# An attention and soft-MoE kernel whose first 27 microseconds are put in another order

## The chip, the cores and the metric

The kernel runs on one core of a Trainium2 chip. A core has a matrix engine (TensorE, here PE, with its weight loads shown apart as PEld), a vector engine (VectorE, DVE), a scalar engine (ScalarE, ACT), GpSimd (POOL) and a queue (SyncE, SP) from which this kernel issues all its transfers. The five run on their own and meet only at semaphores; each takes its own instructions strictly in the order written. The metric is the device time of one execution in microseconds (us), the median of several runs.

## The reference

Eight batches with eight heads of 576 tokens and 64 channels: causal attention with a decay, and then a soft mixture of experts on its output.

```python
scores = scale * q @ k.T
cum    = cumsum(log(clip(f, 1e-4, 1)))
scores = where(causal, -1e9, scores + cum[:, None] - cum[None, :])
attn   = softmax(scores, -1)
x      = concat_heads(attn @ v)                 # 4608 x 512
logits = x @ phi                                # 32 slots, 4 for each of 8 experts
slots  = softmax(logits, 0).T @ x               # dispatch
slots  = relu(slots @ w1[e]) @ w2[e]            # each expert its own 4 slots
out    = softmax(logits, 1) @ slots             # combine
```

## The kernel before

**Tiling.** Two heads of one batch make a pair; there are 32 pairs (numbered g), 64 heads (numbered i), and 5 blocks of 128 tokens for each head. The transposed q and k of a pair come in one load, `RAW` (three buffers, `load_qk`). A product in float32 is made of rounded parts: `round_k` and `round_q` (ACT, lines L183 and L188) write the rounded values of one head to `WA` and `YA`; `dup_k` and `dup_q` copy these to the other half of the partitions of `WB` and `YB` by transfers inside the core (L199, L203); `low_k` and `low_q` (POOL, L209, L214) write what the rounding lost beside them. `WA` and `YA` have three buffers (pairs g, g+3, ... share one), `WB` and `YB` two. The rows 64 and up of `WA` hold the running sum of log f, rounded and its rest; those of `YA` hold constants and, last, the row maximum. For later pairs the sums go to memory (`cumd`, L581) and come back with `load_cum` (L194).

**A head's way.** `s1` (PE, L230) makes the scores with queries on the partitions, into one of three PSUM buffers `s`; `tops` (DVE, L243) masks them and takes each query's maximum. `mturn` (PE, L253) and `mrows` (ACT copy L262, then a transfer L265) turn the maxima into a row of `YA`. `s2` (PE, L280 and L281) makes the scores again, with keys on the partitions and the maximum taken off, into a ring of three PSUM banks; `expo` (ACT, L287) takes the exponential into `PTS`; `causal` (POOL, L295 and L298) zeroes what the mask forbids, the first instruction for three blocks on the diagonal and two more for the last two. `s3` (PE, L313) multiplies with the values `V`; `norm` (DVE, L328 to L333) divides into `X`; `px` and `xcopy` (PE L340, ACT L376 and L349) transpose that for the logits.

**The order of the work** is written out by hand, engine by engine, by the order of the calls; nothing reorders it. A loop over g from 1 to 31 (L722) is one slot for each pair. In slot g, pair g has `s2`, `expo`, `causal` and `s3`, heads 2g+3 and 2g+4 (u0, u1) have `s1` and `tops`, POOL makes the `low` parts of pair g+1, transfers duplicate pair g+2, and ACT rounds pair g+3 (four casts: two heads, k and q). On ACT a slot's order is: three `expo` of the first head, two `xcopy`, its last `expo`, the first `expo` of the second head, three `xcopy`, two `expo`, the `mrows` copy, the last `expo`, and then the four roundings.

**The opening**, L535 to L688, does by hand what the slots before would have done: the running sum (DVE, L562), pairs 0 to 3 rounded, heads 0 to 4 through `s1` and `tops` (`first(i, n)`, n from 0 to 3 for four groups of blocks), pair 0 through everything. The maxima of heads 0 and 1 take their own way (`first_rows`, L603 and L606). `warm(n, ...)` (L527) issues n matmuls whose result nobody reads.

## Time and profile before

| | |
|---|---|
| median of 3 runs | 390.36 us (390.32 to 391.53) |
| the profiled execution | 391.48 us, of which 389.8 us from its first to its last instruction |
| PE busy | 370.1 us (95%) |
| DVE, ACT, POOL busy | 297.5, 269.9, 251.6 us (76%, 69%, 65%) |
| mean granted clock of TensorE | 0.982 |

Times in the trace are microseconds from the first instruction. A row of a timeline gives the start, the length, the engine, the line, what is written and read, how many instructions are merged in it, and in brackets how long the engine was idle before and what ended that. A row of the windows gives busy time and instructions of each engine in a stretch, the granted clock, the share of the transfer engines and the rate. An engine that is busy all the time in a stretch sets that stretch's length; one that is idle may still be the one for which the others wait.

### The profile page before, as it was taken

To read this page: it belongs to the slowest core of one execution; us is meant where nothing else is said; L and a number is where in the kernel's file an instruction comes from. 1 tells how busy PE (TensorE), PEld (TensorE's weight loads), DVE (VectorE), ACT (ScalarE), POOL (GpSimd) and SP (SyncE) were. 2 spreads that over 40 slices of the span, in tenths; PEclk is the share of its full clock that TensorE was granted. 3 is DMA by queue.
4 is the path that set the end of the run, shared out by engine and by line. 5 is a ranking of instruction groups with operands and counts; after the bars stand their busy time and mean duration, and the time that the engine had idled before them with its cause. 6 is when DMAs were issued, how large, how long until landed. Compare 5 with 4: busy or idle time off the path is not lost.

```text
span 389.8 us, 15241 instructions
## 1 busy us (share of the span) xinstructions
PE 370.1 (95%) x5881; PEld 327.9 (84%) x5881; DVE 297.5 (76%) x1161; ACT 269.9 (69%) x685; POOL 251.6 (65%) x339
## 2 busy tenths in 40 slices
...
GB/s 206 230 153 161 172 189 208 200 199 243 243 197 224 216 236 218 218 209 216 215 211 215 215 213 213 220 208 220 211 183 159 309 341 385 409 408 373 270 358 345
DMA packets 34120, 93.72 MB, mean 240 GB/s; under 512 B 4234, under 2 KB 10048, under 8 KB 34048
## 3 DMA queue, kind: packets, MB, share of 16 engines
...
## 4 chain that ended last, share of the span: by engine, by line
PE 79%; DMA 11%; POOL 3%; ACT 3%; DVE 2%; issue 1%; DVEq 0%; SPq 0%; ACTq 0%; POOLq 0%
PE pv L313 25%; PE ring L280 14%; PE ring L281 12%; PE s L230 11%; DMA w<-in_w 7%; PE pv L340 4%; PE lg L387 2%; PE ds L490 2%; POOL YB L214 1%; DMA out<-p 1%; DMA RAW<-in_qk 1%; PE pv L969 1%; PE ring L490 1%; ACT PTS L287 1%; DMA out<-RAW 1%
## 5 line engine op out<-in xcount | busy, mean ns | idle before, releaser
L287 ACT ACTIVATE PTS<-ring 128x320 f32<-128x320 f32 (+2 forms) x256 | 118.1, 502 | 50.2 <-PE ring L281 39.8
L243 DVE CUSTOM_DVE_ANT_0 s<-s,mask 128x320 f32<-128x320 f32 (+4 forms) x320 | 138.5, 452 | 6.1 <-PE s L230 1.0
L280 PE MATMUL ring<-YA,WA 67*128 67x320 f32 (+9 forms) x384 | 119.5, 325 | 0.0
L281 PE MATMUL ring<-YB,WB 128*128 128x320 f32 (+4 forms) x384 | 110.7, 296 | 0.0
L313 PE MATMUL pv<-V,PTS 128*64 128x65 f32 x3200 | 101.9, 223 | 0.9 <-POOL PTS L295 0.5
L209 POOL TENSOR_TENSOR WB<-RAW,WB 64x576 fp32r<-64x576 f32 x64 | 91.0, 1423 | 15.9 <-DMA YA<-V 5.3
L313 PEld LDWEIGHTS pv<-V,PTS 128*64 128x64 f32 x3200 | 97.1, 138 | 4.7 <-issue 1.2
L230 PE MATMUL s<-WA,YA 66*128 66x288 f32 (+9 forms) x384 | 100.4, 317 | 0.4 <-DVE MT L243 0.3
L214 POOL TENSOR_TENSOR YB<-RAW,YA 64x576 fp32r<-64x576 f32 x64 | 89.7, 1420 | 2.5
L280 PEld LDWEIGHTS ring<-YA,WA 67*128 67x128 f32 (+3 forms) x384 | 68.9, 181 | 5.3 <-issue 1.6
L281 PEld LDWEIGHTS ring<-YB,WB 128*128 128x128 f32 (+1 forms) x384 | 69.9, 182 | 0.0
L230 PEld LDWEIGHTS s<-WA,YA 66*128 66x128 f32 (+1 forms) x384 | 63.0, 191 | 5.3 <-DVE MT L243 0.5
L243 DVE DVE_READ_ACCUMULATOR2_ANT MT<- 128x1 f32 x372 | 52.7, 142 | 0.0
L298 POOL TENSOR_SCALAR_AFFINE_SELECT PTS<-PTS 128x128 f32<-128x128 f32 (+1 forms) x128 | 31.3, 265 | 29.9 <-ACT PTS L287 26.4
L295 POOL TENSOR_SCALAR_AFFINE_SELECT PTS<-PTS 128x384 f32<-128x384 f32 x64 | 33.3, 520 | 18.2 <-ACT PTS L287 14.1
L183 ACT CAST WA<-RAW 64x576 fp32r<-64x576 f32 x64 | 40.0, 669 | 4.0 <-DMA RAW<-in_qk 3.4
L340 PE MATMUL pv<-cs,X 128*128 128x128 f32 x155 | 42.1, 273 | 0.6 <-DVE X L333 0.6
L188 ACT CAST YA<-RAW 64x576 fp32r<-64x576 f32 x64 | 40.0, 669 | 0.4
L243 DVE CUSTOM_DVE_ANT_0 s<-s,mask,MT 128x288 f32<-128x288 f32 x62 | 32.6, 526 | 9.6 <-PE s L230 1.0
L333 DVE TENSOR_TENSOR X<-pv,rl 128x320 f32<-128x320 f32 (+1 forms) x65 | 31.5, 486 | 2.4 <-DMA V<-in_v 0.3
L376 ACT COPY XTS<-pv 128x128 f32<-128x128 f32 (+1 forms) x93 | 25.3, 307 | 1.1 <-PE pv L340 0.8
L340 PEld LDWEIGHTS pv<-cs,X 128*128 128x128 f32 x155 | 21.9, 142 | 1.5 <-DVE X L333 0.9
...
## 6 DMA issues: line engine op xcount, KB each, us to landing
...
```

The source lines that it names most:

```text
L183: nc.scalar.copy(WA[g % 3][0:64, S * h : S * h + S], RAW[g % 3][64:128, h])
L188: nc.scalar.copy(YA[g % 3][0:64, h, 64:640], RAW[g % 3][0:64, h])
L209: nc.gpsimd.tensor_tensor(t[0:64], RAW[g % 3][64:128, h], t[64:128].bitcast(F32), op=ALU.subtract)
L214: nc.gpsimd.tensor_tensor(YB[g % 2][64:128, h], RAW[g % 3][0:64, h], YA[g % 3][0:64, h, 64:640].bitcast(F32), op=ALU.subtract)
L230: nc.tensor.matmul(t[:, o : o + w], ya[0:m, h, 128 * blk : 128 * blk + 128], wa[0:m, j0 : j0 + w], start=True, stop=True)
L243: nc.vector.tensor_tensor_reduce(out=t[:, o : o + w], in0=t[:, o : o + w], in1=mask[:, m0 : m0 + w], scale=1.0, scalar=top if n == 3 else ...
L280: nc.tensor.matmul(o, wa[0:m, j0 : j0 + n], ya[0:m, h, 64 + i0 : 64 + i0 + w], start=True, stop=False)
L281: nc.tensor.matmul(o, wb[:, j0 : j0 + n], yb[:, h, i0 : i0 + w], start=False, stop=True)
L287: nc.scalar.activation(PT[i % 2][:, SEG_O[bank] : SEG_O[bank] + at], t[:, 0:at], AF.Exp, scale=0.125)
L295: nc.gpsimd.affine_select(d3, d3, pattern=[[0, 3], [1, 128]], compare_op=ALU.is_ge, fill=0.0, base=0, channel_multiplier=-1)
L313: nc.tensor.matmul(pvv[h][64 * u : 64 * u + 64, t, :], PT[h][:, at : at + 64], V[:, g % 2, c, 65 * h : 65 * h + 65], start=(c == 0), stop= ...
L340: nc.tensor.transpose(pm[:, 0:128], x[:, t, 128 * (p % 2) : 128 * (p % 2) + 128], ident)
```

## The change

Only the opening and slots 1 and 2 differ; from slot 3 on the programs are the same. The constants for `YA` and `WA` are prepared in `XTS` in place of `V`. For head 1 the two rows of running sums go to `WA` by two transfers in place of two ACT copies. The roundings of pair 1's first head are done together and early, those of its second head inside pair 0's `expo`; pairs 1 and 2 are duplicated head by head, pair 1's first head right behind `load_v(0)`. `load_qk(3)` is issued later. `first(2, ...)` and `first(3, ...)` are put between products of pair 0; `s3` of pair 0 is cut into four parts with `first(3, 2)`, `first(3, 3)` and `first(4, 0)` between. `low_q(2)` comes ahead of `causal(1)`. The last two groups of head 4 and the four roundings of pair 3 move into slot 1, `own_j` (two DVE instructions) into slot 2. Three of the 24 `warm` matmuls are left out.

```diff
-    fill = V.rearrange("p a t c -> p (a t c)")[:, 0:1280].bitcast(F32R)
+    fill = XTS[:, 0:1280].bitcast(F32R)
...
+    def fills(m, n):
+        if n == 0:
+            nc.sync.dma_start(WA[m][66:67].bitcast(F32), fill[0:1, 0 : 2 * S].bitcast(F32))
+        else:
+            nc.sync.dma_start(YA[m][64:66].rearrange("c h s -> c (h s)").bitcast(F32), fill[32:34].bitcast(F32))
+
     nc.vector.tensor_copy(fp[lane, 0:S], fz)
+    nc.sync.dma_start(WA[0][64:65, S:].bitcast(F32), fp[96:97, 0:S].bitcast(F32))
+    dup_k(0, 1, 2)
+    fills(1, 0)
...
+    nc.sync.dma_start(WA[0][96:97, S:].bitcast(F32), fp[96:97, S:].bitcast(F32))
+    for c in range(2):
+        nc.sync.dma_start(WA[1][64 + c : 65 + c].bitcast(F32), fp[65:98:32, S * c : S * c + S].bitcast(F32))
+    fills(1, 1)
+    nc.scalar.copy(WA[0][64:65, 0:S], fp[64:65, 0:S])
     round_q(0, 1)
-    nc.scalar.activation(fin[:, 0:1], ones[:, 0:1], AF.Exp)
     dup_q(0, 1, 2)
+    nc.sync.dma_start(cumd.rearrange("b a c s -> (b a) (c s)"), fp[lane].bitcast(F32))
+    fills(2, 0)
+    fills(2, 1)
     load_qk(2)
     load_v(0)
+    nc.scalar.activation(fin[:, 0:1], ones[:, 0:1], AF.Exp)
...
     round_k(1, 0)
+    round_q(1, 0)
+    dup_k(1, 0, 1)
+    dup_q(1, 0, 1)
...
-    first(1, 1, 3 * WARM[1])
+    first(1, 1, 2 * WARM[1])
+    first(1, 2)
     next(r0)
-    warm(2 * WARM[1], cs)
     next(r0)
-    round_q(1, 0)
-    first(1, 2)
+    round_k(1, 1)
+    first(1, 3, WARM[1])
     both(0, 0)
-    first(1, 3)
+    first(2, 0)
     both(0, 1)
+    round_q(1, 1)
+    dup_k(1, 1, 2)
+    dup_q(1, 1, 2)
...
     causal(0)
     low_k(2)
+    low_q(2)
+    first(2, 3, 2 * WARM[1])
     both(1, 0)
...
     both(1, 3)
+    round_k(2, 0)
+    round_q(2, 0)
+    dup_q(2, 0, 1)
+    dup_k(2, 0, 1)
     causal(1)
-    low_q(2)
     low_k(3)
     low_q(3)
+    s3(0, alone[0][:13])
+    first(3, 2)
+    s3(0, alone[0][13:])
+    first(3, 3)
     nc.vector.memset(most, -1.0e30)
-    s3(0, alone[0])
+    s3(0, alone[1][:13])
     first(4, 0)
+    s3(0, alone[1][13:])
     mturn(1, 1, 2)
     mrows(1, 1, 2)
+    round_k(2, 1)
+    round_q(2, 1)
+    dup_q(2, 1, 2)
+    dup_k(2, 1, 2)
     first(4, 1)
     norm(0)
     load_cum(3)
-    round_k(3)
-    round_q(3)
...
         expo(h0, 0)
+        if g == 1:
+            first(4, 2)
         norm(h0 - 1)
...
         expo(h0, 1)
+        if g == 1:
+            first(4, 3)
...
         expo(h0, 2)
+        if g == 1:
+            round_k(3, 0)
+            round_q(3, 0)
         px(g - 1, 0)
...
         expo(h1, 0)
+        if g == 1:
+            round_k(3, 1)
+            round_q(3, 1)
```

How this stands on the engines, at the three places that matter below. First POOL, from the end of pair 0's `causal(0)` (the last `PTS` row of 64 columns) on; `WB_88`, `YB_87` are the low parts of pair 1, `PTS` the exponentials. Before:

```order
L209 TENSOR_TENSOR WB_88<-RAW_96,WB_88 64x576
L295 AFFINE_SELECT PTS<-PTS 128x3x128
L298 AFFINE_SELECT PTS<-PTS 128x128
L298 AFFINE_SELECT PTS<-PTS 128x64
L214 TENSOR_TENSOR YB_87<-RAW_96,YA_85 64x576
```

and now:

```order
L209 TENSOR_TENSOR WB_88<-RAW_96,WB_88 64x576
L214 TENSOR_TENSOR YB_87<-RAW_96,YA_85 64x576
L295 AFFINE_SELECT PTS<-PTS 128x3x128
L298 AFFINE_SELECT PTS<-PTS 128x128
L298 AFFINE_SELECT PTS<-PTS 128x64
```

The q part of head 2 has moved ahead of head 1's mask. Second ACT, from the last two `expo` of head 1 to slot 1's copies of `X` (`WA_94`, `YA_93` are pair 2, `WA_90`, `YA_89` pair 3, `mr_1` the maxima of head 3). Before:

```order
L287 ACTIVATE PTS<-ring_151 128x512
L188 CAST YA_93<-RAW_97 64x576 x2
L262 CAST mr_1_408<-pv_148 5x128
L183 CAST WA_90<-RAW_95 64x576 x2
L188 CAST YA_89<-RAW_95 64x576 x2
L287 ACTIVATE PTS<-ring_149 128x448
L287 ACTIVATE PTS<-ring_150 128x320
L287 ACTIVATE PTS<-ring_151 128x320
L376 COPY XTS<-pv_147 128x128 x2
L287 ACTIVATE PTS<-ring_149 128x512
L287 ACTIVATE PTS<-ring_150 128x448
L376 COPY XTS<-pv_148 128x2x128
```

and now, from the maxima of head 3 on:

```order
L262 CAST mr_1_430<-pv_148 5x128
L183 CAST WA_94<-RAW_97 64x576
L188 CAST YA_93<-RAW_97 64x576
L287 ACTIVATE PTS<-ring_149 128x448
L287 ACTIVATE PTS<-ring_150 128x320
L287 ACTIVATE PTS<-ring_151 128x320
L183 CAST WA_90<-RAW_95 64x576
L188 CAST YA_89<-RAW_95 64x576
L376 COPY XTS<-pv_147 128x128 x2
L287 ACTIVATE PTS<-ring_149 128x512
L287 ACTIVATE PTS<-ring_150 128x448
L183 CAST WA_90<-RAW_95 64x576
```

The four casts of pair 3 stood ahead of slot 1's first `expo`, and stand among its `expo` now; behind the copy of head 3's maxima there are two casts of pair 2. Third PE, the end of the opening up to slot 1's first product (`YA_85`, `WA_86` with L280). Before:

```order
L313 MATMUL pv_147<-V,PTS 64x65 x25
L230 MATMUL s_0_402<-WA_94,YA_93 128x320
L230 MATMUL s_0_402<-WA_94,YA_93 128x192
L253 MATMUL pv_148<-cs,MT_113 5x128
L230 MATMUL s_1_413<-WA_94,YA_93 128x288
L313 MATMUL pv_148<-V,PTS 64x65 x13
L230 MATMUL s_2_429<-WA_94,YA_93 128x288
L230 MATMUL s_3_436<-WA_94,YA_93 128x448
L230 MATMUL s_3_436<-WA_94,YA_93 128x64
L313 MATMUL pv_148<-V,PTS 64x65 x12
L280 MATMUL ring_149<-YA_85,WA_86 128x448
```

and now:

```order
L313 MATMUL pv_148<-V,PTS 64x65 x13
L230 MATMUL s_0_412<-WA_94,YA_93 128x320
L230 MATMUL s_0_412<-WA_94,YA_93 128x192
L313 MATMUL pv_148<-V,PTS 64x65 x12
L253 MATMUL pv_148<-cs,MT_113 5x128
L230 MATMUL s_1_437<-WA_94,YA_93 128x288
L280 MATMUL ring_149<-YA_85,WA_86 128x448
L281 MATMUL ring_149<-YB_87,WB_88 128x448
L230 MATMUL s_2_452<-WA_94,YA_93 128x288
```

The transposition of head 3's maxima (L253) stood between the values of head 0 and those of head 1, and stands behind both now; the last products of head 4 follow slot 1's first product.

## The prediction

> **What bounds the kernel now.** I read the busy time by stretches cut at the slots' starts first, then the timelines of PE, POOL, ACT and SP over the first 55 us.

> ```profile
> 26.80:36.90 10.10, 9.32 (x147) 8.51 (x143) 8.36 (x35) 7.31 (x18) 9.70 (x12) 1.00 0.62 161
> 36.90:45.70 8.80, 8.77 (x144) 8.38 (x143) 7.20 (x30) 7.16 (x18) 7.95 (x11) 1.00 0.61 169
> ```

> The columns behind the length are PE, PEld, DVE, ACT and POOL, the clock, the transfers' share and rate. In slot 2 PE is busy 8.77 of 8.80 us: PE sets it and, with 95% of the whole span, what follows; whatever shifts slot 2 shifts everything behind it. In slot 1 (26.8 to 36.9) PE lacks 0.8 us and POOL is busy 9.7 of 10.1. So the change is worth what it does to the start of slot 2. PE's timeline up to there:

> ```profile
> 10.38 0.53 PE L230 MATMUL s<-WA,YA 97*128 97x320 f32 x2
> 18.37 0.50 PE L280 MATMUL ring<-YA,WA 98*128 98x448 f32 x1
> 23.09 0.51 PE L230 MATMUL s<-WA,YA 66*128 66x320 f32 x2
> 23.43 0.27 PE L253 MATMUL pv<-cs,MT 128*5 128x128 f32 x1
> 24.21 1.26 PE L313 MATMUL pv<-V,PTS 128*64 128x65 f32 x26 [0.37 <-POOL PTS L295]
> 25.41 0.63 PE L230 MATMUL s<-WA,YA 66*128 66x288 f32 x3
> 25.97 0.92 PE L313 MATMUL pv<-V,PTS 128*64 128x65 f32 x24
> 26.82 0.47 PE L280 MATMUL ring<-YA,WA 67*128 67x448 f32 x1
> 28.96 0.33 PE L340 MATMUL pv<-cs,X 128*128 128x128 f32 x1 [0.59 <-DVE X L333]
> 33.33 1.50 PE L313 MATMUL pv<-V,PTS 128*64 128x65 f32 x42
> 35.00 1.96 PE L313 MATMUL pv<-V,PTS 128*64 128x65 f32 x58 [0.17 <-POOL PTS L295]
> 36.89 0.47 PE L280 MATMUL ring<-YA,WA 67*128 67x448 f32 x1
> 45.66 0.47 PE L280 MATMUL ring<-YA,WA 98*128 98x448 f32 x1
> ```

> Slot 1 starts at 26.82, slot 2 at 36.89, slot 3 at 45.66: slot 1 takes 10.07 us, slot 2 8.77. At 24.21 and again at 35.00 PE waits for POOL's mask, at 28.96 for `norm`. POOL's rows say why the mask is late:

> ```profile
> 9.83 1.41 POOL L209 TENSOR_TENSOR WB<-RAW,WB 64x576 fp32r<-64x576 f32 x1 [5.31 <-DMA YA<-V]
> 11.31 1.41 POOL L214 TENSOR_TENSOR YB<-RAW,YA 64x576 fp32r<-64x576 f32 x1
> 22.16 1.40 POOL L209 TENSOR_TENSOR WB<-RAW,WB 64x576 fp32r<-64x576 f32 x1 [5.12 <-DMA YB<-YA]
> 23.64 0.52 POOL L295 TENSOR_SCALAR_AFFINE_SELECT PTS<-PTS 128x384 f32<-128x384 f32 x1
> 34.42 0.52 POOL L295 TENSOR_SCALAR_AFFINE_SELECT PTS<-PTS 128x384 f32<-128x384 f32 x1
> ```

> It stands idle 5.12 us before `low_k(2)` at 22.16, which needs `dup_k(1)`; a `low` part takes 1.48 from start to start (9.83, 11.31). PE follows a mask's start by 0.57 (23.64 to 24.21) or 0.58 (34.42 to 35.00).

> **The change part by part.** First the duplicate. ACT and SP now:

> ```profile
> 7.20 1.36 ACT L583 CAST WA<-PTS 1x576 fp32r<-1x576 f32 x2
> 9.40 0.67 ACT L188 CAST YA<-RAW 64x576 fp32r<-64x576 f32 x1
> 11.61 0.67 ACT L183 CAST WA<-RAW 64x576 fp32r<-64x576 f32 x1
> 5.81 0.52 SPq L199 DMA_DIRECT2D WB<-WA  x1
> 12.90 0.58 SPq L174 DMA_DIRECT2D RAW<-in_qk  x1
> 17.96 0.48 SPq L199 DMA_DIRECT2D WB<-WA  x1
> 0.80 2.75 DMA PTS<-in_f
> 15.73 3.96 DMA RAW<-in_qk
> ```

> With two of three row copies gone, ACT reaches `round_q(0,1)` at 7.20 + 0.68 = 7.9 instead of 9.4; pair 1's first head, at 11.61 before, is rounded by 11.5 in both parts. SP now decides. From `dup_k(0,0)` at 5.81 to `load_qk(2)` at 12.90 it issues 11 transfers, 0.645 each; `dup_k(1,0)` is the 15th behind the same start, so it is issued at 5.81 + 15 x 0.645 = 15.5 at the latest, and at 14.8 with 0.6 for each: I take 15.2, for the longest of the steps before held waits. `load_qk(2)` itself slips from 12.90 to some 14.1; its first reader, a cast, stands behind head 1's last `expo`, so nothing waits.

> How long the transfer takes has two rows: `dup_k(0,0)`, 5.81 to 9.83, 4.0 us, and `dup_k(1)`, 17.96 to 22.16, 4.2 us, both behind loads. An early end is the 2.75 us of the first load, which had the queue to itself; a late one adds up what is ahead: `load_qk(2)` (576 KB, as the load at 15.73) lands 3.96 after its issue, at 18.1, and behind it come 325 KB and the duplicate's own 144 KB. The transfer engines are nearly full there already (0.87, at 273 GB/s, the last two columns):

> ```profile
> 18.00:20.00 2.00, 2.00 (x15) 1.90 (x14) 1.72 (x9) 1.46 (x3) 0.00 (x0) 1.00 0.87 273
> ```

> At that rate these 469 KB are 1.7 us: 19.8. So the duplicate lands between 18.0 and 19.8; I take 15.2 + 4.2 = 19.4, the row that is nearest in kind. `low_k(2)` then starts 2.76 us earlier than at 22.16.

> [...]

> Of these 2.76 us `causal(1)` gets only part, since `low_q(2)` now stands ahead of it: 19.4 + 2 x 1.48 = 22.35 against 23.64, and PE may go on with head 1's values at 22.35 + 0.57 = 22.9 against 24.21. PE is there by then: `s2` of head 1 starts with the copies of head 1's maxima, now 0.67 later by the cast put in before them:

> ```profile
> 16.51 0.73 ACT L606 CAST YA<-ring 2x512 fp32r<-2x512 f32 x2 [0.16 <-PE ring L603]
> 23.79 0.25 ACT L262 CAST mr<-pv 5x128 fp32r<-5x128 f32 x1 [0.17 <-PE pv L253]
> 25.33 1.25 ACT L188 CAST YA<-RAW 64x576 fp32r<-64x576 f32 x2
> 27.53 1.31 ACT L287 ACTIVATE PTS<-ring 128x448 f32<-128x448 f32 x3 [0.95 <-PE ring L281]
> 29.68 0.43 ACT L376 COPY XTS<-pv 128x128 f32<-128x128 f32 x2 [0.84 <-PE pv L340]
> 30.75 1.03 ACT L287 ACTIVATE PTS<-ring 128x512 f32<-128x512 f32 x2 [0.64 <-PE ring L281]
> 31.67 0.38 ACT L376 COPY XTS<-pv 128x256 f32<-128x256 f32 x1
> 32.38 0.77 ACT L287 ACTIVATE PTS<-ring 128x320 f32<-128x320 f32 x2
> ```

> 16.51 + 0.73 + 0.67 = 17.9, and from there to the end of head 0's values the same work took 18.37 to 23.09, 4.72: 22.6. From 24.21 to 26.82, 2.61 us, PE did head 1's values and two groups of head 4 (25.41 to 25.97, 0.56); these go, and the first group (23.09 to 23.43, 0.34), the transposition (0.03) and the second group (0.14) come: 2.56. **Slot 1 starts at 22.9 + 2.56 = 25.5, 1.4 us earlier.**

> Slot 1 then gives it back on ACT. Before, ACT had rounded pair 3 by 26.6 (25.33 + 1.25) and stood idle 0.95 us when `expo(2,0)` came at 27.53. Now the copy of head 3's maxima waits for a transposition that stands behind all of head 1's values, and two casts of pair 2 are queued behind the copy. The transposition starts at 22.9 + 1.20 + 0.34 + 0.85 = 25.3 and the copy follows by 0.36 (23.43 to 23.79): 25.65. Then in order: the copy 0.25, two casts 1.25, three `expo` 1.31, two casts 1.25, two copies 0.43, two `expo` 1.03, two casts 1.25, three copies 0.71 (31.67 to 32.38), two `expo` 0.77. That is 8.25 us, 8.33 with the 0.01 or so between two, without a wait: 33.98. Before, ACT waited 0.84 and 0.64 for PE inside this slot (29.68, 30.75); the added casts stand just there and fill most of it. I take 0.3 for what is left, with bounds of 0 and 0.9: 34.28. The mask follows at once, POOL being through by 33 (five `low` parts of 1.48 and `causal(2)` behind `causal(1)`): start 34.28, PE goes on 0.58 later at 34.86 where it was 35.00. **Slot 2 starts 0.14 us earlier than at 36.89**; with the bounds of the landing and of ACT's waits, from 0.7 earlier to 0.9 later.

> What costs nothing, and what covers it: `own_j` in slot 2

> ```profile
> 22.65 0.94 DVE L672 TENSOR_SCALAR own_j<-own_j 128x4 f32<-128x4 f32 x1
> 35.80 0.17 DVE L328 TENSOR_SCALAR rl<-pv 128x5 f32<-128x5 f32 x1 [0.96 <-PE pv L313]
> 44.67 0.17 DVE L328 TENSOR_SCALAR rl<-pv 128x5 f32<-128x5 f32 x1 [0.82 <-PE pv L313]
> ```

> stands, with a shorter instruction ahead of it, 1.2 us in all, where DVE waited 0.82 us for the values; the other 0.4 moves `norm(4)`, whose reader on PE comes some 1.5 us into the slot. Without that cover it would cost 1.2. `first(4,2)` and `first(4,3)` cost slot 1 0.56 us of PE, which waits there for ACT anyway, and on DVE at most 1.8 (a slot's 7.20 hold eight such groups and two `norm`); DVE starts on the slot 1.4 earlier and waited 0.96 behind it (35.80). Head 1's two row transfers, issued at about 7.0 and 8.9 by SP's pace, land by 11.6 with the 2.75 us of the first load and could hold PE's `s1` of head 1, at 10.38 before, for 1.2; DVE, which reads it, is busy with head 0 for about half of that, so I count 0.6 at most, and the 0.3 between PE's 22.6 and POOL's 22.9 hide half. The three `warm` matmuls stood where PE waits anyhow. The sum against the profile's own 391.48 is -0.14, which gives 391.3; that run is 0.3% above the median of the runs, so the forecast is 390.36 - 0.14, **390.2 us**, no change: a measurement of this kernel can tell 0.3%, 1.2 us.

> **The rivals.** *PE sets slot 1.* If ACT's waits vanish and its casts hide, slot 1 takes PE's own 8.77 + 0.56 = 9.3 us from 25.5: slot 2 at 34.8, 2.1 earlier, **388.3 us**. For it speaks that ACT had 0.95 + 0.84 + 0.64 = 2.4 us idle about slot 1, nearly the 2.5 that it gets; against it, that the 0.95 lay before `expo(2,0)`, where ACT now waits for the maxima's copy.

> *ACT sets slots 1 and 2.* The landing at 19.8 and waits of 0.9 put slot 2 at 37.9; ACT then ends its last `expo` and the four roundings of pair 4 at about 38.9, and slot 2's first `expo` starts 1.0 behind its product. It decides from the point where that `expo` ends after PE's want of the bank for the fourth product, some 1.8 us into the slot; then PE waits 0.5 more: 1.5 later, **391.8 us**. For it speaks that ACT's 7.16 us in slot 2 leave 1.6 to catch up, and no more; against it, that the landing must be at its late end.

> *The row transfers are late.* Head 1's `s1` starts 0.6 later and the chain to 22.6 with it: 0.3 us lost, 390.5, the same verdict.

> **How the numbers follow.** ACT's chain as summed 0.55, PE sets slot 1 0.24, ACT sets two slots 0.17, late rows 0.04. The forecast's own range, 0.7 earlier to 0.9 later, is 389.7 to 391.3; I widen it to hold the faster rival and stop short of the slower: 388.2 to 391.7. Faster by over 0.3% (below 389.2): the second with 0.02 of the first, 0.26; slower: 0.17; within 0.3%: 0.57.

> **What would show it.** `low_k(2)` at 19.4 (18.0 to 19.8), `causal(1)` at 22.4, slot 1's first product at 25.5; ACT idle from about 22 until the copy of head 3's maxima near 25.7; no more than 0.3 us idle on ACT from there to its last `expo` of slot 1; PE's stop for the mask in slot 1 longer than 0.17; slot 2 at 36.8 and slots 2 and 3 unchanged in length. Wrong if ACT's casts find idle time (slot 1 near 9.3 us), if `low_k(2)` still waits past 20, or if slot 2 is longer than 8.8.

## The result and the profile after

| | before | changed |
|---|---|---|
| median | 391.53 us (390.32 to 400.96, 11 runs) | 394.57 us (392.58 to 395.82, 11 runs) |
| ratio | | 1.0087, 95% interval 1.0064 to 1.0109: slower |
| profiled execution | 391.48 us, span 389.8 | 395.82 us, span 394.1 |
| mean granted clock of that execution | 0.982 | 0.972 |

The forecast was 390.2 us, no change, with a range up to 391.7; the kernel became 0.9% slower and lies outside it. Part of the distance is no term of the prediction: the forecast started from 390.36, the median of three runs, and the kernel before took 391.53 in these eleven. Runs more than 1.5% above the fastest of their kernel are left out of the ratios: 400.96 and 399.50 here, and one of e20_thin below, 398.43. The runs of the changed kernel differ from each other by the clock: the three with a mean granted clock of 0.982 or more took 392.6 to 393.1 us, the eight others, at 0.972 to 0.981, 394.3 to 395.8. So two things have to be found: some 1.1 to 1.6 us that are lost at full clock, and up to 3 us more that come with a lower clock.

PE's timeline of the changed kernel at the places that answer to those shown of before:

```profile
24.05 1.26 PE L313 MATMUL pv<-V,PTS 128*64 128x65 f32 x26 [0.75 <-POOL PTS L295]
26.78 0.37 PE L280 MATMUL ring<-YA,WA 67*128 67x448 f32 x1
28.57 0.40 PE L230 MATMUL s<-WA,YA 66*128 66x288 f32 x1 [1.08 <-ACT YA L188]
37.03 4.99 PE L313 MATMUL pv<-V,PTS 128*64 128x65 f32 x100
41.95 0.47 PE L280 MATMUL ring<-YA,WA 67*128 67x448 f32 x1
```

Head 1's values start at 24.05 (22.9 was predicted, 24.21 before), slot 1 at 26.78 (25.5; 26.82), slot 2 at 41.95 (36.75; 36.89). The opening gained nothing, and slot 1 takes 15.2 us in place of 10.1. At 28.57 stands a stop of 1.08 us that the prediction did not have: `s1` of head 5 waits for a cast of pair 2. And a hundred products for the values take 4.99 us, where in other executions below they take 3.14. The windows, cut at steps of the clock, show why (columns as before; the ninth number, 0.50, is the granted clock):

```profile
27.43:30.84 3.41, 2.33 (x17) 2.09 (x17) 3.23 (x17) 2.70 (x6) 2.91 (x3) 1.00 0.35 75
30.84:34.25 3.41, 3.41 (x17) 3.17 (x16) 2.75 (x13) 3.00 (x7) 1.49 (x4) 0.50 0.82 265
34.25:37.66 3.41, 3.41 (x26) 3.16 (x27) 2.27 (x9) 2.79 (x9) 1.27 (x2) 0.50 0.07 28
37.66:41.07 3.41, 3.41 (x68) 3.41 (x66) 0.63 (x5) 2.62 (x5) 3.05 (x4) 0.50 0.55 107
```

TensorE runs at half clock from 30.84 to 41.07, three windows of 3.41 us, all with PE busy to the last. The window ahead of them holds the stop of 1.08 us. Before, the clock was 1.00 here, from 26.80 to 45.70.

Of the 5.06 us by which slot 2 is late, 4.3 are left at the end (394.1 against 389.8): the execution before had a half-clock window of its own, 3.41 us at 324.38, which the changed one had not.

POOL and SP show where the opening's gain went:

```profile
20.54 1.41 POOL L209 TENSOR_TENSOR WB<-RAW,WB 64x576 fp32r<-64x576 f32 x1 [2.55 <-PE ring L281]
22.00 1.41 POOL L214 TENSOR_TENSOR YB<-RAW,YA 64x576 fp32r<-64x576 f32 x1
23.48 0.52 POOL L295 TENSOR_SCALAR_AFFINE_SELECT PTS<-PTS 128x384 f32<-128x384 f32 x1
```

```profile
14.26 0.39 SPq L174 DMA_DIRECT2D RAW<-in_qk  x1
14.70 0.43 SPq L178 DMA_DIRECT2D V<-in_v  x1
15.24 0.48 SPq L199 DMA_DIRECT2D WB<-WA  x1
```

The duplicate is issued at 15.24, as predicted, but POOL starts `low_k(2)` at 20.54 and not at 19.4. The name behind the arrow is of an operation long done: the wait is for the duplicate, which by its semaphore landed at 20.37, 5.1 us after its issue. And ACT in front of slot 1:

```profile
26.88 0.26 ACT L262 CAST mr<-pv 5x128 fp32r<-5x128 f32 x1 [4.37 <-PE pv L253]
27.16 0.67 ACT L183 CAST WA<-RAW 64x576 fp32r<-64x576 f32 x1
27.84 0.67 ACT L188 CAST YA<-RAW 64x576 fp32r<-64x576 f32 x1
28.42 0.53 ACT L287 ACTIVATE PTS<-ring 128x448 f32<-128x448 f32 x1
```

ACT stands idle 4.37 us for the maxima of head 3, and the two casts of pair 2 that had no need to wait are queued behind: the second ends at 28.5, and with it PE's stop. DVE waits as well. `tops` (L243) of the last two groups of head 3 starts at 20.99 and 21.43 before, the first of them behind 0.20 us in which DVE waits for the product of L230; in the changed kernel at 21.83 and 23.34, behind 1.25 and 0.93 us of waiting for L230.

With parts of pair 0's values ahead of the score products of heads 3 and 4, DVE waits for these products, and the last group comes 1.9 us later.

### The profile page after: what moved, and what is told of

Same layout as the page of the kernel before. It is cut to its first block, busy times and chain, and to the rows that moved or that the text cites. A ratio compares the mean times of both kernels' runs of the same rounds, so it can differ in the third digit from the quotient of the medians.

```text
span 394.1 us, 15235 instructions
## 1 busy us (share of the span) xinstructions
PE 372.8 (95%) x5875; PEld 330.0 (84%) x5875; DVE 297.7 (76%) x1161; ACT 269.1 (68%) x683; POOL 252.1 (64%) x339
## 4 chain that ended last, share of the span: by engine, by line
PE 84%; DMA 6%; ACT 3%; issue 1%; POOL 1%; DVE 1%; SPq 0%; DVEq 0%; ACTq 0%; POOLq 0%
PE pv L313 24%; PE ring L280 14%; PE ring L281 12%; PE s L230 11%; PE pv L340 4%; PE pv L987 3%; PE lg L387 2%; PE ds L490 2%; PE ring L950 2%; PE pv L950 2%; DMA YA<-mr 2%; DMA YB<-YA 1%; ACT PTS L287 1%; DMA out<-p 1%; PE ring L987 1%
## 5 line engine op out<-in xcount | busy, mean ns | idle before, releaser
L287 ACT ACTIVATE PTS<-ring 128x320 f32<-128x320 f32 (+2 forms) x256 | 118.5, 502 | 53.0 <-PE ring L281 38.9
L243 DVE CUSTOM_DVE_ANT_0 s<-s,mask 128x448 f32<-128x448 f32 (+4 forms) x320 | 138.6, 451 | 9.6 <-PE s L230 4.5
L280 PE MATMUL ring<-YA,WA 67*128 67x320 f32 (+9 forms) x384 | 120.4, 327 | 0.6 <-DMA YA<-mr 0.4
L281 PE MATMUL ring<-YB,WB 128*128 128x320 f32 (+4 forms) x384 | 111.8, 299 | 0.0
L313 PE MATMUL pv<-V,PTS 128*64 128x65 f32 x3200 | 103.7, 225 | 1.1 <-POOL PTS L295 0.8
L230 PE MATMUL s<-WA,YA 66*128 66x288 f32 (+9 forms) x384 | 102.0, 321 | 1.6 <-ACT YA L188 1.1
L313 PEld LDWEIGHTS pv<-V,PTS 128*64 128x64 f32 x3200 | 98.8, 140 | 4.7 <-issue 1.2
L209 POOL TENSOR_TENSOR WB<-RAW,WB 64x576 fp32r<-64x576 f32 x64 | 91.1, 1423 | 13.6 <-DMA WB<-WA 6.0
L214 POOL TENSOR_TENSOR YB<-RAW,YA 64x576 fp32r<-64x576 f32 x64 | 89.7, 1420 | 2.4
L280 PEld LDWEIGHTS ring<-YA,WA 67*128 67x128 f32 (+3 forms) x384 | 69.8, 183 | 6.2 <-issue 1.6
L281 PEld LDWEIGHTS ring<-YB,WB 128*128 128x128 f32 (+1 forms) x384 | 70.9, 185 | 0.0
L230 PEld LDWEIGHTS s<-WA,YA 66*128 66x128 f32 (+1 forms) x384 | 64.1, 193 | 7.1 <-ACT YA L188 1.4
L243 DVE DVE_READ_ACCUMULATOR2_ANT MT<- 128x1 f32 x372 | 52.5, 141 | 0.0
L295 POOL TENSOR_SCALAR_AFFINE_SELECT PTS<-PTS 128x384 f32<-128x384 f32 x64 | 33.5, 523 | 22.0 <-ACT PTS L287 16.9
L183 ACT CAST WA<-RAW 64x576 fp32r<-64x576 f32 x64 | 40.2, 669 | 3.3 <-DMA RAW<-in_qk 2.5
L340 PE MATMUL pv<-cs,X 128*128 128x128 f32 x155 | 42.4, 274 | 0.0
L243 DVE CUSTOM_DVE_ANT_0 s<-s,mask,MT 128x288 f32<-128x288 f32 x62 | 32.6, 526 | 11.0 <-PE s L230 2.9
L188 ACT CAST YA<-RAW 64x576 fp32r<-64x576 f32 x64 | 40.2, 669 | 0.4
L333 DVE TENSOR_TENSOR X<-pv,rl 128x320 f32<-128x320 f32 (+1 forms) x65 | 31.5, 486 | 2.4 <-DVE rl L329 0.3
L376 ACT COPY XTS<-pv 128x128 f32<-128x128 f32 (+1 forms) x93 | 25.2, 306 | 0.3
L340 PEld LDWEIGHTS pv<-cs,X 128*128 128x128 f32 x155 | 22.1, 143 | 0.7
```

Of the source, the lines that this page charges most:

```text
L183: nc.scalar.copy(WA[g % 3][0:64, S * h : S * h + S], RAW[g % 3][64:128, h])
L188: nc.scalar.copy(YA[g % 3][0:64, h, 64:640], RAW[g % 3][0:64, h])
L209: nc.gpsimd.tensor_tensor(t[0:64], RAW[g % 3][64:128, h], t[64:128].bitcast(F32), op=ALU.subtract)
L214: nc.gpsimd.tensor_tensor(YB[g % 2][64:128, h], RAW[g % 3][0:64, h], YA[g % 3][0:64, h, 64:640].bitcast(F32), op=ALU.subtract)
L230: nc.tensor.matmul(t[:, o : o + w], ya[0:m, h, 128 * blk : 128 * blk + 128], wa[0:m, j0 : j0 + w], start=True, stop=True)
L243: nc.vector.tensor_tensor_reduce(out=t[:, o : o + w], in0=t[:, o : o + w], in1=mask[:, m0 : m0 + w], scale=1.0, scalar=top if n == 3 else ...
```

## The experiments

All numbers: median, and ratio to the kernel before on the same chip with its 95% interval. The rows come from several chips, so rows are compared by their ratios. "Changed" means that the edit is made to the changed kernel.

| label | edit | median us | ratio |
|---|---|---|---|
| e2_maxima | changed, head 3's maxima ahead of head 1's values | 397.02 | 1.0173 (1.0143 to 1.0204) |
| e3_mask | changed, `causal(1)` ahead of `low_q(2)` | 393.58 | 1.0084 (1.0054 to 1.0114) |
| e10_casts | changed, pair 2's casts ahead of the maxima's copy | 394.23 | 1.0077 (1.0048 to 1.0105) |
| e11_casts_mask | e10 and e3 together | 395.39 | 1.0121 (1.0075 to 1.0168) |
| e14_round3 | e10, pair 3's roundings in the opening | 393.66 | 1.0082 (1.0055 to 1.0109) |
| e7_order_mask | changed, heads 3 and 4 as before; e3 | 391.16 | 1.0004 (0.9985 to 1.0024) |
| e12_round30 | e7, two of pair 3's casts in the opening | 391.87 | 1.0036 (1.0021 to 1.0051) |
| e16_place | e12, the other two where ACT is idle | 389.98 | 0.9981 (0.9965 to 0.9996) |
| e18_ahead | e16, one group of head 4 ahead of head 1's values | 389.53 | 0.9968 (0.9949 to 0.9987) |
| e19_two | before, two casts of pair 3 into slot 1 | 393.12 | 1.0057 (1.0037 to 1.0077) |
| e15_early | before, the early part of the change and e3 | 390.20 | 0.9986 (0.9976 to 0.9995) |
| e17_rows | e15, head 1's sums by ACT copies | 390.31 | 0.9992 (0.9970 to 1.0013) |
| e1_fill | changed, idle products in PE's stops, one bank | 395.43 | 1.0135 (1.0098 to 1.0172) |
| e9_fill | changed, idle products, other bank | 393.47 | 1.0069 (1.0044 to 1.0095) |
| e13_thin | e9 with 2 rows of 128 | 394.93 | 1.0105 (1.0082 to 1.0127) |
| e5_idle | before, 1.2 us of useless DVE work | 391.75 | 1.0034 (1.0006 to 1.0063) |
| e20_thin | before, eight idle products of 2 rows | 393.17 | 1.0043 (1.0026 to 1.0059) |
| e21_full | before, the same with 128 rows | 392.59 | 1.0034 (1.0023 to 1.0046) |

### Single edits of the changed kernel

**e2_maxima.** The two lines move up:

```diff
+    mturn(1, 1, 2)
+    mrows(1, 1, 2)
     s3(0, alone[1][:13])
     first(4, 0)
     s3(0, alone[1][13:])
-    mturn(1, 1, 2)
-    mrows(1, 1, 2)
```

> The changed kernel with the transposition and the copy of head 3's maxima put back ahead of head 1's values, so that the casts of pair 2's second head no longer queue behind them. Clock theory: ACT's 4.4 us idle shrinks to about 2, PE's wait of 1.08 for the cast at 28.57 goes, the busy share of that stretch rises and the clock stays at 1.00: 390 to 391.5, level with or below the kernel before. Order theory: about 1 us less than the change, 393.5. If the clock falls all the same, the wait for the mask at 24.05 is enough to bring it down.

It became worse, 397.02, which neither theory had. In the profiled execution half clock holds from 27.0 for 13.65 us, and PE stops in two other places ahead of it:

```profile
24.53 0.27 PE L253 MATMUL pv<-cs,MT 128*5 128x128 f32 x1 [1.11 <-DVE LGM L681]
25.28 1.23 PE L313 MATMUL pv<-V,PTS 128*64 128x65 f32 x26 [0.48 <-ACT mr L262]
```

The transposition waits for DVE, which is late with head 3 because `first(3, 3)` stands behind the values of head 0; then the values of head 1 wait for the copy, since both use one bank. So with heads 3 and 4 where the change puts them, moving the maxima ahead only moves the stop; slot 1 starts at 28.70 in place of 26.78, in part by the half clock.

**e3_mask.** `causal(1)` goes ahead of `low_q(2)` on POOL.

```diff
     low_k(2)
-    low_q(2)
...
     causal(1)
+    low_q(2)
     low_k(3)
```

> The changed kernel with causal(1) back ahead of low_q(2) on POOL. The mask starts at about 22.0 in place of 23.48, PE's wait of 0.75 at 24.05 goes and slot 1 starts some 0.9 earlier; PE's wait of 1.08 in slot 1 for the cast stays, since the maxima's copy and the casts keep their order. Clock theory: the stretch that decides (27.4 to 30.8) then holds other work, so the clock may or may not fall; if it falls, about 393.5 to 394.5, if not 390.5 to 391.5. Order theory: 0.9 less than the change, 393.7.

The mask came at 21.99 and the stop of 0.75 at 24.05 was gone; slot 1 started at 26.09. The stop in slot 1 stayed:

```profile
27.89 0.40 PE L230 MATMUL s<-WA,YA 66*128 66x288 f32 x1 [1.09 <-ACT YA L188]
```

Its runs took 392.4 to 395.9 at clocks of 0.985 to 0.971. What the order on POOL costs is less than this spread, and 393.58 lies where both theories had it.

**e10_casts, e11_casts_mask, e14_round3.** Pair 2's casts ahead of the copy; then also the mask; then, in place of the mask, pair 3's roundings behind these casts and not in slot 1.

```diff
+    round_k(2, 1)
+    round_q(2, 1)
+    round_k(3)           # e14 alone
+    round_q(3)           # e14 alone
     mturn(1, 1, 2)
     mrows(1, 1, 2)
-    round_k(2, 1)
-    round_q(2, 1)
```

> The changed kernel with the two casts of pair 2's second head ahead of the copy of head 3's maxima on ACT, nothing else. Theory A (the loss is the queue on ACT behind the copy, and the half clock that the stop of s1(5,1) brings): ACT casts at 22.5 to 23.9 in its idle 4.37 us, PE's stop of 1.08 us before s1(5,1) in slot 1 is gone, slot 1 still starts near 26.8, slot 2 near 36.4, the granted clock is 1.00 from 27 to 41, and the time is 390.0 to 391.2. Theory B (the starved DVE, with the products of heads 3 and 4 behind pair 0's values, sets slot 1): the stop only changes its releaser and the time stays above 392.

> The same with causal(1) ahead of low_q(2) as well, so that no stop over 0.4 us is left in the opening behind 20. Theory A: slot 1 starts at 26.1 in place of 26.8, slot 2 near 35.8, 0.6 us better than with the casts alone: 389.5 to 390.6. Theory B: no better than the casts alone, over 392.

> The changed kernel with the casts of pair 2's second head ahead of the maxima's copy (394.23; 392.1 to 392.5 in runs at 0.982) and the four roundings of pair 3 behind these, in the opening, where ACT stood idle 2.3 us. Theory A: no cast is left inside slot 1, ACT's chain there is 2.7 us shorter and starts 0.5 later; PE's stop of 1.16 us at 34.4 is gone, and runs at 0.982 take 390.9 to 391.5. Theory B (the products of heads 3 and 4 behind pair 0's values starve DVE and that alone costs over 1 us): they stay above 392.

e10's stops in slot 1:

```profile
28.67 0.40 PE L230 MATMUL s<-WA,YA 66*128 66x288 f32 x1 [0.67 <-DVE rl L328]
35.56 1.62 PE L313 MATMUL pv<-V,PTS 128*64 128x65 f32 x48 [1.16 <-ACT mr L262]
```

The stop for the cast is gone, and a stop of 0.67 for DVE stands at the next score product of head 5; PE waits 1.16 us for the copy of the maxima (L262) in front of the slot's values. (That row counts only the products up to 37 us; all hundred take 3.14 us. The rows of e7 and e19 below end early in the same way.) Its runs at full clock took 392.1 to 392.5, the others up to 396.4. Theory A's 390.0 to 391.2 was wrong: the casts behind the copy made the stop of 1.08, and behind it stood another, for the starved DVE. In e14's profiled execution, which ran slot 1 at half clock, PE does not wait in front of the slot's values; what is left is 0.80 us before head 1's values and

```profile
28.68 0.40 PE L230 MATMUL s<-WA,YA 66*128 66x288 f32 x1 [0.66 <-DVE rl L328]
```

Its two runs at the highest clock took 391.75 and 391.78, between the two theories' numbers. e11's four runs were all at a clock of 0.974 or less, 394.2 to 398.2, where theory A had 389.5 to 390.6: slot 1 starts at 25.76, a microsecond earlier than in the changed kernel, but the stop of 0.67 for DVE stays at 27.81 and half clock follows: the product of L280 with 448 columns at 30.49 takes 0.72 us, its like in e9, at 31.90 and a clock of 1.00, 0.45.

### The order of heads 3 and 4, and the place of pair 3's casts

**e7_order_mask** puts the groups of heads 3 and 4 back; roundings, duplicates, sums and slot 1 stay changed.

```diff
+    first(3, 2)
+    first(3, 3)
     round_k(2, 0)
...
-    s3(0, alone[0][:13])
-    first(3, 2)
-    s3(0, alone[0][13:])
-    first(3, 3)
...
-    s3(0, alone[1][:13])
+    s3(0, alone[0])
     first(4, 0)
-    s3(0, alone[1][13:])
     mturn(1, 1, 2)
...
     first(4, 1)
+    s3(0, alone[1])
     norm(0)
```

> The changed kernel with the groups of heads 3 and 4 back where they stood against pair 0's values (first(3,2) and first(3,3) ahead of them, head 3's maxima ahead of head 1's values), and causal(1) ahead of low_q(2). What stays of the change: early and separate roundings and duplicates, sums by transfers, roundings of pair 3 and two groups of head 4 in slot 1. Theory A: the maxima's copy comes near 24 and the casts behind it are done by 25.5, no stop over 0.6, full clock, slot 1 at 25.5 to 26.1, slot 2 near 35.3: 388.8 to 390.2. Theory B expects the same here or better than the casts alone by over 1 us, since DVE is fed again; so the two differ in whether this beats the kernel with casts and mask by more than 1 us. If the late duplicate itself is the loss, head 1's values still start at 23.5 or later and the time is over 391.

391.16, level with before, and every run at a clock of 0.981 or more. From e3 it differs in this order alone, and is faster by 0.8% of the time (1.0004 against 1.0084). So the order, `s3` pieces ahead of the products that DVE waits for, with the clock that follows from it, is the largest part of the loss. It is lost inside slot 1: slot 1 starts at 25.77 here and at 25.76 in e11, but PE's stops for the cast and for DVE are gone. Theory A had put the casts first and was wrong in that: this beats the kernel with casts and mask by far more than 1 us, as theory B had it. Head 1's values start at 23.91 and the time is over 391, as expected if the late duplicate were the loss; but they wait there 0.35 us for the copy of head 3's maxima, and the mask had come at 22.26. One stop is left:

```profile
34.17 3.02 PE L313 MATMUL pv<-V,PTS 128*64 128x65 f32 x96 [1.17 <-ACT mr L262]
```

**e12_round30, e16_place.** Two of pair 3's four casts go to the opening (e12); then the other two from behind `expo(h1, 0)` to behind `expo(h0, 2)` (e16).

```diff
     dup_k(2, 1, 2)
+    round_k(3, 0)
+    round_q(3, 0)
     first(4, 1)
...
         expo(h0, 2)
         if g == 1:
-            round_k(3, 0)        # e12
-            round_q(3, 0)
+            round_k(3, 1)        # e16
+            round_q(3, 1)
...
         expo(h1, 0)
-        if g == 1:               # e16
-            round_k(3, 1)
-            round_q(3, 1)
```

> The kernel with the old order of heads 3 and 4 and the earlier mask (391.16, whose PE stops 1.17 us at 33.0 behind ACT), with the roundings of pair 3's first head moved from slot 1 into the opening, behind pair 2's, where ACT had 1.34 us idle. Theory A (ACT sets slot 1, as predicted, by the four casts put into it): ACT's chain in the slot is 1.3 us shorter, the stop of 1.17 is down to 0.2 or less, slot 2 starts about 0.9 us earlier: 389.9 to 390.6, at the granted clock of 0.985. Theory C (slot 1 is set by something else, such as DVE or POOL's low parts): the stop stays within 0.3 us of 1.17 with another releaser, and the time stays at 391.

> The kernel with one pair of pair 3's casts in the opening (391.87) and the other pair moved from behind expo(h1,0) to behind expo(h0,2) in slot 1, where ACT stood idle 0.69 and 0.65 us. If the place of these two casts, 1.35 us right ahead of the slot's last exponentials with no idle time left behind them, makes the stop of 1.20 us before slot 1's values, the stop is down to 0.3 or less, slot 1's values start at 33.0 to 33.3 in place of 34.2, and the time is 390.2 to 390.9. If ACT's sum over the slot decides, whatever the order, the stop stays over 0.8 and the time at 391.5 or more.

Taking two casts away (e12) brought nothing, where theory A had 389.9 to 390.6: 391.87, stop 1.20, slot 2 at 37.27 as in e7 (37.24). ACT's timeline says which two:

```profile
28.02 0.44 ACT L287 ACTIVATE PTS<-ring 128x320 f32<-128x320 f32 x1 [0.50 <-PE ring L281]
29.15 0.44 ACT L376 COPY XTS<-pv 128x128 f32<-128x128 f32 x2 [0.69 <-PE pv L340]
30.23 1.03 ACT L287 ACTIVATE PTS<-ring 128x512 f32<-128x512 f32 x2 [0.65 <-PE ring L281]
31.29 0.67 ACT L183 CAST WA<-RAW 64x576 fp32r<-64x576 f32 x1
31.97 0.67 ACT L188 CAST YA<-RAW 64x576 fp32r<-64x576 f32 x1
33.26 0.77 ACT L287 ACTIVATE PTS<-ring 128x320 f32<-128x320 f32 x2
```

The casts that were taken out had only filled the 0.69 and 0.65 us that are idle here at 29.15 and 30.23. The two that stayed stand at 31.29, where no wait is left between them and the last exponential: all of their 1.35 us reach it. e16 put these two into the idle time, with the same sum of work, and the values start without a stop, 1.2 us earlier:

```profile
33.02 3.13 PE L313 MATMUL pv<-V,PTS 128*64 128x65 f32 x100
36.09 0.47 PE L280 MATMUL ring<-YA,WA 67*128 67x448 f32 x1
```

389.98 us. The place of the casts decides, not ACT's sum.

**e19_two.** The same two casts alone, in the kernel before.

```diff
     load_cum(3)
-    round_k(3)
-    round_q(3)
+    round_k(3, 0)
+    round_q(3, 0)
...
         expo(h1, 0)
+        if g == 1:
+            round_k(3, 1)
+            round_q(3, 1)
```

> The kernel before with the two casts of pair 3's second head moved from the end of the opening to behind expo(h1,0) of slot 1, nothing else. ACT's first exponential of slot 1 comes at 27.2 in place of 27.5, and the slot's last ones about 1.0 us later; PE's stop before slot 1's values grows from 0.17 to 1.0 to 1.3 us. If the stop reaches the end: 391.3 to 391.9 against 390.6 to 391.1. If ACT's idle time inside the slot (0.84 and 0.64) takes the casts in, as the prediction summed it: no difference to before.

```profile
35.04 4.18 PE L313 MATMUL pv<-V,PTS 128*64 128x65 f32 x81 [1.42 <-ACT mr L262]
```

393.12, over 2 us lost, where 391.3 to 391.9 was expected: the stop grew from 0.17 to 1.42 and in the profiled execution a window of half clock followed it (35.48 to 38.89).

**e18_ahead.** From e16, one group goes to where PE waits for the copy of head 3's maxima.

```diff
     first(4, 1)
+    first(4, 2)
     s3(0, alone[1])
...
         expo(h0, 0)
-        if g == 1:
-            first(4, 2)
```

> The kernel of e16_place with the third group of head 4 taken out of slot 1 and put ahead of head 1's values, where PE waits 0.35 us for the copy of head 3's maxima out of the bank that the values are written to. The group takes about 0.3 us of PE: the stop is filled, slot 1 starts at the same time and is 0.3 us shorter on PE: 0.2 to 0.4 us below e16_place if PE sets the slot, the same if ACT does.

389.53, 0.3% below the kernel before: the best of all, and better than both kernels. Its interval and e16's overlap, so that the group alone is worth 0.45 us isn't shown. Slot 1's values and slot 2 start at

```profile
32.57 3.14 PE L313 MATMUL pv<-V,PTS 128*64 128x65 f32 x100 [0.17 <-ACT mr L262]
35.64 0.47 PE L280 MATMUL ring<-YA,WA 67*128 67x448 f32 x1
```

1.25 us ahead of 36.89.

### The early part alone

**e15_early** is the kernel before with the roundings and duplicates by heads, the sums by transfers, the groups of heads 1 and 2 moved up, and `causal(1)` ahead of `low_q(2)`; `own_j` is in slot 2. From e7 that takes:

```diff
     dup_k(2, 1, 2)
     first(4, 1)
-    s3(0, alone[1])
+    s3(0, alone[1][:13])
+    first(4, 2)
     norm(0)
+    first(4, 3)
+    s3(0, alone[1][13:])
     load_cum(3)
+    round_k(3)
+    round_q(3)
```

and nothing of pair 3 or head 4 in slot 1. **e17_rows** then puts head 1's sums back to ACT copies:

```diff
-    nc.sync.dma_start(WA[0][64:65, S:].bitcast(F32), fp[96:97, 0:S].bitcast(F32))
...
-    nc.sync.dma_start(WA[0][96:97, S:].bitcast(F32), fp[96:97, S:].bitcast(F32))
-    nc.scalar.copy(WA[0][64:65, 0:S], fp[64:65, 0:S])
+    for h in range(2):
+        nc.scalar.copy(WA[0][64:65, S * h : S * h + S], fp[64 + 32 * h : 65 + 32 * h, 0:S])
+    nc.scalar.copy(WA[0][96:97, S:], fp[96:97, S:])
```

> The kernel before with the early part of the change alone (roundings and duplicates of pairs 1 and 2 by heads, sums by transfers, groups of heads 1 and 2 moved up) and the mask ahead of low_q(2); heads 3 and 4 and pair 3's roundings stand as before. Theory A: PE's stop of 0.37 at 24.2 goes, slot 1 starts up to 0.5 earlier, but ACT rounds pair 3 until 27.5 as before and its first exponential of the slot comes no earlier, so nothing reaches slot 2: 390.6 to 391.3, no difference. If the duplicate had been what bound the opening, it would be 390.2 or less.

> The kernel with the early part alone (390.20) with head 1's two rows of sums by ACT copies again, as in the kernel before. The stop of 0.49 us at 10.7 before head 1's products goes. ACT is 1.3 us later with the roundings, but SP has two transfers less ahead of dup_k(1,0), which is issued near 14.5 or, if the rounding is late, at 15.3. If the row transfers cost what PE waited: 389.7 to 390.1. If DVE or the copies of head 0's maxima set that stretch and not PE: 390.1 to 390.5, no difference.

e15 took 390.20, 0.14% below before, its interval ending at 0.9995: a small gain, less than the 0.3% that the prediction called tellable. The time meets "390.2 or less", but the kernel before took 390.59 on this chip, so the ratio has to decide. Theory A's "nothing reaches slot 2" was wrong: slot 2 starts 0.8 us earlier than before:

```profile
33.02 3.14 PE L313 MATMUL pv<-V,PTS 128*64 128x65 f32 x100
36.09 0.47 PE L280 MATMUL ring<-YA,WA 67*128 67x448 f32 x1
```

In e17 PE's stop at 10.7 was gone (0.49 us in e15), and SP issued the duplicate 1.2 us earlier, yet POOL could start hardly earlier:

```profile
14.02 0.48 SPq L199 DMA_DIRECT2D WB<-WA  x1
```

```profile
20.36 1.42 POOL L209 TENSOR_TENSOR WB<-RAW,WB 64x576 fp32r<-64x576 f32 x1 [2.66 <-PE ring L281]
```

20.36 in place of 20.53; in the fourteen profiles with the duplicate issued at 15.2 to 15.3 this start lies between 20.36 and 21.17. `load_qk(2)`, issued 1.2 us earlier too, also landed only 0.2 us earlier (18.20 against 18.39). So here the landing does not follow the issue; that it is held by the traffic ahead of it fits, and was not tested by taking that traffic away. The row transfers cost nothing that shows in the time, though slot 2 starts at 35.72 in this profile, 0.37 earlier.

### The clock

**e5_idle** puts DVE work of 1.2 us that nothing needs ahead of `norm(1)` in the kernel before, to make PE wait there.

```diff
         expo(h0, 0)
+        if g == 1:
+            nc.vector.tensor_reduce(own_j[:, 0], ident.rearrange("p (j s) -> p j s", j=4), axis=AX.X, op=ALU.add)
+            nc.vector.tensor_scalar(own_j[:, 1], own_j[:, 0], 1.0e30, -1.0e30, op0=ALU.mult, op1=ALU.add)
         norm(h0 - 1)
```

> The kernel before with 1.2 us of DVE work of no use ahead of norm(1) in slot 1, so that PE's wait of 0.59 at 28.96 becomes about 1.8. Clock theory: TensorE is granted half its clock from 30.8 on for at least 3.4 us, and the time rises by 2.5 to 6 us, more than the 1.2 put in. Order theory: it rises by 1.2 at most, and less if PE's 0.2 and DVE's 0.96 of slack behind it take some.

Six of ten runs had a mean clock of 0.984 or more and took 390.7 to 391.9, as before; four, at 0.974 to 0.981, took 392.3 to 395.1. The loss comes with the clock, and only in some runs. But e5 does not test the stop that it was made for: in its profiled execution PE does not wait at `norm(1)`, and the half clock, 27.35 to 30.76, follows a stop ahead of the added work,

```profile
25.42 1.26 PE L313 MATMUL pv<-V,PTS 128*64 128x65 f32 x26 [1.32 <-POOL PTS L295]
```

because `low_k(2)` started at 23.37. In the five profiles with the old opening (before, e5, e19, e20, e21) that start lies between 21.77 and 23.37, with the duplicate issued at 17.9 to 18.0 in all of them.

**e1_fill, e9_fill, e13_thin.** Products whose result nobody reads, in PE's two long stops of the changed kernel: e1 four and six of them into bank 0, e9 three and four into bank 1; e13 is e9 with operands of 2 rows.

```diff
+    def keep_busy(n):
+        for _ in range(n):
+            nc.tensor.matmul(pv[1][:, 454:510], cs[:, 0:128], cs[:, 0:56], start=True, stop=True)
...
+    keep_busy(3)
     s3(0, alone[1][:13])
...
             first(4, 2)
+            keep_busy(4)
```

> The changed kernel with ten short products that nobody reads put where PE waits: four ahead of head 1's values, six behind the third group of head 4 in slot 1. Clock theory (PE's waits in the stretch before 30.8 us make the chip halve TensorE's clock for 10.24 us, and that is most of the loss): the clock stays at 1.00 to 300 us, slot 2 starts at 37 to 38 in place of 41.95, and the time falls by 3 to 5 us in the runs where the change had the half clock, to 391 to 392.5. Order theory (the loss is the waits of ACT and POOL themselves, the clock a by-product): the same waits are there, so the time stays within 1 us of the change.

> The changed kernel with products that nobody reads where PE stood idle: three before head 1's values (0.75 us) and four behind first(4,2) in slot 1 (1.0 us), written to a bank whose reader is not waited for there. Theory A on the clock: no idle stretch is left that brings the half clock, so every run shows a mean granted clock of 0.98 or more and the time is 392.0 to 392.9, that is the loss of order alone. If the drops have nothing to do with PE's idle time, runs at 0.97 and 395 stay.

> The kernel with idle products (393.47 us, clock 0.981 to 0.987), with the same products reading 2 rows of their operands in place of 128: same columns, same durations, same stops left, but 1/64 of the array's rows active. If the granted clock is cut by PE's idle time, this behaves as the full products did: clock 0.981 or more in every run, 393.0 to 393.9. If it is cut by how much of the array works (in the profiles so far every window of 3.41 us whose moved columns, weighted by active rows of 128, came to less than 2,700 was followed by half clock, and none above 2,840), the stops filled so count as idle and the runs are as without them: most at 0.977 or less and 394.3 to 396.5.

e1 failed as a test: its products wait for DVE's reading of that bank and made a new stop,

```profile
28.25 1.54 PE L624 MATMUL pv<-cs 128*128 128x56 f32 x12 [0.85 <-DVE X L333]
```

e9 filled most of the two stops (0.36 and 0.24 us are left). Its four runs show clocks of 0.981 to 0.987, but 393.4 to 394.7 us, at least 0.5 more than expected; and in the profiled one half clock still came, from 36.58 to 39.99, behind a stop of 1.38 us in front of slot 1's values, which the products did not fill. In e13, with the same columns and no idle time left, two of six runs fell to 0.972 and 0.976, less than the "most" that the second theory expected. Its profile shows the point. The window with the filled stop, first of e9, then of e13:

```profile
26.34:29.75 3.41, 3.17 (x42) 2.92 (x38) 3.05 (x14) 2.07 (x5) 3.35 (x3) 1.00 0.07 20
29.75:33.16 3.41, 3.28 (x25) 2.79 (x24) 3.34 (x15) 3.04 (x8) 1.33 (x2) 1.00 0.69 153
```

```profile
26.58:29.99 3.41, 3.34 (x34) 2.88 (x31) 3.05 (x15) 2.35 (x5) 3.20 (x3) 1.00 0.11 26
29.99:33.41 3.42, 3.42 (x18) 3.34 (x18) 2.80 (x13) 2.22 (x6) 0.92 (x2) 0.50 0.88 229
```

With PE busy 3.34 of 3.41 us, more than in e9 (3.17), half clock follows: 0.50 from 29.99.

**e20_thin, e21_full** put it to the test in the kernel before: eight such products in slot 1, with 2 rows and with 128.

```diff
         expo(h0, 0)
+        if g == 1:
+            keep_busy(8)        # into pv[0]; e20: cs[0:2, ...], e21: cs[:, ...]
         norm(h0 - 1)
```

> The kernel before with eight products that nobody reads, about 2.05 us by the profiles so far, behind the first exponential of slot 1; they read 2 rows of their operands. PE is not idle there any more than before (0.59 us at most). Theory W (the clock follows the work of the array: columns moved, weighted by active rows): the window of 3.41 us that holds them falls from about 3,600 to 1,750 to 2,400, under 2,700, half clock follows for 3.4 to 10 us in most runs, and the time is 1.5 us of added work and 1.5 to 4 more: 393.5 to 396, mean clock 0.971 to 0.980. Theory I (the clock follows PE's idle time): no drop, clock 0.984, 391.7 to 392.5.

> The same eight products reading all 128 rows: the same columns, the same place and time. Both theories: no half clock in the opening, 0.984 and 391.7 to 392.5, the added 1.5 us alone. So theory W expects e20_thin 1.5 to 4 us above this kernel, theory I the same time within 0.4.

e20, then e21:

```profile
27.00:30.42 3.42, 3.42 (x33) 2.98 (x30) 2.39 (x10) 0.55 (x2) 3.36 (x4) 1.00 0.97 182
30.42:33.83 3.41, 3.41 (x19) 3.33 (x18) 2.01 (x9) 1.31 (x4) 1.57 (x2) 0.50 0.63 248
33.83:37.24 3.41, 3.41 (x14) 3.08 (x15) 1.98 (x9) 2.72 (x8) 1.99 (x4) 0.50 0.01 2
```

```profile
27.59:31.00 3.41, 3.41 (x27) 3.27 (x28) 2.58 (x11) 1.09 (x3) 3.35 (x3) 1.00 0.91 207
31.00:34.41 3.41, 3.41 (x29) 3.26 (x28) 3.20 (x15) 2.70 (x10) 3.25 (x6) 1.00 0.55 180
```

In e20 PE is busy for the whole window and half clock follows for 6.8 us; in e21, busy for just as long, it does not. e21's twelve runs kept 0.982 or more; of six of e20 three fell to 0.977 and 0.978 (393.2 to 394.9 us), three stayed at 0.982 (392.1 to 392.8). Theory I is out: in e20 the drop came without idle time of PE. That the drop costs 1.5 us or more in most runs did not hold; it was half of them, and the median of the six, 392.98, is 0.4 above e21's.

What goes with the drop can be read off these profiles to some degree. For each window of 3.41 us on the grid of the clock's steps (in the kernel before they lie at 324.38, 327.79 and 378.99, which is 3.41 and 51.20 apart, 1 and 15 windows), I summed the columns that its matmuls moved, each weighted by its active rows over 128 (a row "66*128 66x448" has 66 rows and 448 columns), each counted in the window in which it starts. Nine of the windows:

| kernel, window from | PE idle us | weighted columns | clock behind it |
|---|---|---|---|
| e20_thin, 27.00 | 0.00 | 1778 | half |
| changed, 27.43 | 1.08 | 2674 | half |
| e13_thin, 26.58 | 0.07 | 2720 | half |
| e9_fill, 22.92 | 0.36 | 2843 | full |
| e19_two, 32.06 | 1.42 | 2914 | half |
| e10_casts, 32.73 | 1.23 | 2984 | full |
| e21_full, 27.59 | 0.00 | 3008 | full |
| e9_fill, 26.34 | 0.24 | 3496 | full |
| before, 27.42 | 0.59 | 3626 | full |

From 10 to 60 us of all twenty profiles, eleven windows at full clock were followed by half, ten of them at 2720 or less and one at 2914; none of the others lies under 2843. Windows at half clock follow nearly the same line: eleven of the twelve that stayed at half came to 2872 or less, the other to 2916, and none of those that returned lay under 2894. Behind 320 us, in the profiles of before and of the changed kernel, three windows at full clock were followed by half, at 1920, 1792 and 1792; the others there lie at 3072 or more. The line had been drawn before e13 was run, from the profiles so far: half below 2700, full above 2840. e20 and e21 then fell as it said, and e19 did not. So it is a good description of the opening in these profiles, not a law; what exactly brings the drop stays open.

## Why the prediction was wrong

**The duplicate (mis-sized).** Its issue, 15.2, was met at 15.24. "Lands between 18.0 and 19.8; I take 19.4" was wrong by 1.0, past its own late end: `load_qk(2)` was counted to land at 18.1 and landed at 18.45, and the 469 KB behind it took 1.9 us and not 1.7. e17 showed that POOL's start stands near 20.4 even with the issue 1.2 us earlier. The late end should have been the value to take. This term carries the miss at slot 1's start: 26.78 in place of 25.5, of which 1.15 were there when head 1's values began. The early end took 2.75 us from a load that did not have the queue to itself: the next was issued at 1.48, 0.68 behind it.

**The mask and PE's arrival (right in kind, late by the same).** `causal(1)` came 2.94 behind the start of `low_k(2)` (2.96 predicted), at 23.48 in place of 22.35; PE was ready at 23.30, not 22.6. Head 1's values started 1.15 later than 22.9.

**"I take 0.3 for what is left, with bounds of 0 and 0.9" (failed).** The new order of heads 3 and 4 was costed on PE's own time, 0.34 and 0.85 us for its pieces, and on ACT's chain, with 0.3 us of waits in slot 1. That DVE waits for these very products, and PE in slot 1 for DVE and for the casts behind the maxima, was put at nothing. This is the step that failed. Ahead of slot 1 it cost 0.2 (2.73 from head 1's values to slot 1, 2.56 predicted). Inside slot 1 PE stopped for 1.08 us, in e10 for 0.67, and ACT stood idle for 1.5 in e10 (0.32 and 1.17) behind the copy. Slot 1 took 12.01 us in e10 at full clock, where the prediction had 11.25, and 11.47 in e7, with the old order. With the clock that follows, the order is worth 0.8% of the time: e7 against e3. At full clock the two misses together put slot 2 of e10 at 38.63 in place of 36.75: 1.1 from slot 1's start, 0.8 inside it.

**The casts behind the maxima's copy (seen, and not followed to its end).** The prediction had the copy, the two casts and ACT's idle time in front of slot 1, and counted them on ACT's chain; it did not ask who else waits for these casts. `s1` of head 5 does, early in PE's queue of slot 1: 1.08 us. The casts were not the only cause of a stop there, as e10 showed.

**ACT sets slot 1 (right in kind).** With the old order of heads 3 and 4 slot 1 took 11.47 us (e7), near the 11.25 that the prediction had added up on ACT. "The added casts stand just there and fill most of it" held for two of four casts. In e10, at full clock, the chain from the copy (26.72) to the values (35.56) took 8.84, where the prediction had 8.33 + 0.3 + 0.58 = 9.2 with the two casts that e10 had moved out of it, 7.9 without; so it was 0.9 longer, with 1.5 us of waits on ACT and not 0.3, while the values followed the last of these exponentials sooner than the 0.58 that was counted. One reason is the place: two casts stand behind the last idle time. e16 and e19 show it from both sides; the other is the step above.

**The clock (missing).** No rival had it. The prediction's tables showed 1.00 throughout, and I took this for safe. It went with 1.2 to 3.2 us more in eight of eleven runs (394.3 to 395.8 against 392.6 to 393.1); in the profiled execution the window with the stop of 1.08 us was followed by 10.24 us at half clock.

**What held.** The row transfers (0.3 at most, nothing measured in e17); of `own_j` no run was made alone, but in e15 and e18, where it stands in slot 2, slots 2 and 3 are of their old length; for one group of head 4 in slot 1, e16 and e18 leave at most some 0.45 us. The slower rival, "ACT sets slots 1 and 2", came nearest: both its conditions were met and passed (landing at 20.4 against 19.8, 1.5 us of waits on ACT in e10 against 0.9), and it had 1.5 us where the runs at full clock lost 1.1 to 1.6. But it put 0.5 of that into slot 2, which took 8.79 us, as before. The three `warm` products were not tried alone.
